# Backward pass of a segment-recurrent attention block: second dO half copied by two engines, tail block's fold moved to the dH fold, tail passes halved, hi parts first in folds

## The chip, the core and the metric

One core of a Trainium2 chip runs the whole program in one launch. The metric is device microseconds of an execution; the kernel before took 3185.75 us in the median of 4 runs (3175.45 to 3195.62). Profiles show one execution: the engines PE (matmul), PEld (its weight loads), DVE, ACT, POOL, and SP, which here only issues DMAs.

## The reference, cut to what matters

The program computes the output of a conditioned transformer block and the gradients of its eleven inputs. The block is layer norm with modulation, a memory-augmented attention over 64 segments of 32 rows each, and a gated MLP. What the change touches is the backward pass of the attention:

```python
for s in range(n_seg):                                   # 64 segments, in the backward pass from 63 down to 0
    h = jnp.concatenate([mem, xs], axis=1)               # 8 memory rows, 32 rows of x: L = 40
    q = jnp.einsum('btd,dhe->bhte', h, Wq)               # k, v likewise; 32 heads of 128
    p = _softmax(jnp.where(mask, einsum(q, k) * scale, -1e9), axis=-1)
    o = jnp.einsum('bhqk,bhke->bhqe', p, v)
    o = jnp.einsum('bhte,hed->btd', o, Wo)
    mem = o[:, :M, :].copy()                             # the next segment's memory
    outs.append(o[:, M:, :])
_out, _vjp = jax.vjp(_f, A_x, A_mem0, A_Wq, A_Wk, A_Wv, A_Wo, B_w_gate, B_w_up, B_w_down, c, w_mod)
```

The gradient of a segment's memory rows is part of the gradient of the output of the segment before it, so the backward pass is a chain of 64 segments.

## The kernel before

The program runs in phases: the forward attention (to about 1010 us of the profile), the MLP forward and backward, the backward attention (`phase4`, 1574 to 2570 us), and the weight gradients. The change is in `phase4` and in helpers that `phase4` calls. `fold_sum` and `TailRows` serve the forward attention's tail blocks too, once in four segments.

`phase4` is one loop over the segments s = 63 to 0. Its instruction order is written out by hand: `self.pin(i0)` keeps each engine in program order, so whatever stands behind a waiting instruction on its engine waits too. A step does this, by name:

- **dO pass.** `col_pass` multiplies the step's gradient columns `dyT` by `WoT`, in two halves `hf` of 16 matmuls; four column groups of PE work side by side. Each half lands in a PSUM tile `pass_ps` and is copied to the row tile `RAd`: half 0 by DVE, half 1 by ACT. POOL copies both on into `dOst` (L1538).
- **Turn.** `turn(0)` and `turn(1)` transpose `RAd` on PE (L1390), each in two tiles `turn_ps`, and ACT and DVE write them into `dOT`.
- **Gradients.** `gv0` and `gv1` are dV products (`grad_mm`, L1509, tiles `g_ps`); `dp`, `ds` give dS (L1488, L1496, L1498); `dost(2)` transposes part of `dOT` (L1424, tiles `tps`). `grad_out` copies a `g_ps` to `dVT`, `dKT` or `dQT`. After the third part, SP transposes the whole tile by DMA into `rows_x` (L1517), and POOL stores that to DRAM. The next step's first copy into `dVT` has to wait until that DMA has read it.
- **dH.** `dht` multiplies `dVT`, `dKT`, `dQT` by the transposed weights into `dh_ps` (L212, 96 matmuls). `fold_split` splits `dh_ps` into bf16 hi parts (ACT, L305) and lo parts (DVE, L309), two halves of 256 columns each, and `fold_sum` adds the four row groups up with 8 small matmuls into `dh_ft` (L318). ACT copies its memory rows into the next step's `dyT` (L1597), which the next dO pass needs.

Work of the **tail rows** (the last 8 rows of each segment, gathered for blocks of four segments) is put between these. `proj_b(t, hf)` is a dO pass over a block's tail rows `dyb`, half 0 in the steps with s % 4 = 3 and half 1 in those with s % 4 = 2, after the fold. `turn_b` transposes its result in the steps with s % 4 = 1. `TailRows` multiplies a block's tail gradients by the three weights (96 matmuls into `dh_tps`): `chunk()` runs one of four pieces of 24 matmuls in each step, between `fold_split` and `fold_sum`. `tail.split()` splits a finished block, in the steps with s % 4 = 3, and its `fold_sum` (`dh_b_ft`) runs in the `pop_later` between the `dKT` and the `dQT` products. `store_rows` copies `dh_ft` into `dh_tb` on DVE (L326) and turns it later (L330).

The loop's PSUM tiles share eight buffers (called banks below): six rotate under the tag "p" of the pool `psp`; `dh_ps` and `dh_tps` have one each, under tags of the pool `psb`. A tile of "p" gets a bank that an earlier tile has left, and its first matmul waits until that tile's last reader is done.

Of the kernel before, what the change touches and what calls it, by code (L numbers as in the profile page):

```python
# [40 lines left out]
class K:  # L41
# [199 lines left out]
    def col_pass(self, psp, w, hf, lhs, rows, eng):  # L241

        E, DC = self.cfg.E, self.cfg.DC
        ps = psp.tile([128, 512], F32, name="pass_ps", tag="p")
        for c in range(DC):
# [52 lines left out]
    def fold_split(self, pool, ps, name, tags=""):  # L298

        nc = self.nc  # L300
        parts = []
        for h in range(2):
            sl = slice(256 * h, 256 * h + 256)
            hi = pool.tile([128, 256], BF16, name=name + "_hi", tag=f"{tags}hi{h}", bufs=1)
            nc.scalar.activation(hi[:], ps[:, sl], AF.Copy)  # L305
            parts.append(hi)
        for h in range(2):
            lo = pool.tile([128, 256], BF16, name=name + "_lo", tag=f"{tags}lo{h}", bufs=1)
            nc.vector.tensor_tensor(lo[:], ps[:, 256 * h:256 * h + 256], parts[h][:], op=ALU.subtract)  # L309
            parts.append(lo)  # L310
        return parts

    def fold_sum(self, psp, parts, name, tag):

        ft = psp.tile([128, self.cfg.DC, 32], F32, name=name + "_ft", tag=tag)
        for c in range(self.cfg.DC):
            for i in range(2):
                self.nc.tensor.matmul(ft[:, c, :], lhsT=parts[2 * i + c // 2][:, (c % 2) * 128:(c % 2) * 128 + 128],  # L318
                                      rhs=self.foldsel[:], start=(i == 0), stop=(i == 1))
# [988 lines left out]
    def phase4(self):  # L1308
# [7 lines left out]
        with self.p4_ctx as ctx:  # L1316
# [76 lines left out]
            def proj_b(t, hf):  # L1393
                ps = self.col_pass(psp, WoT, hf, lambda c: dbs[t][:, c, :, :].rearrange("p s q -> p (s q)"), None, None)
                return lambda: self.evac(("act", "dve")[hf], RBds[t % 2][:, 512 * hf:512 * hf + 512], ps[:])
# [40 lines left out]
            for hf in range(2):  # L1436
                proj_b(NS // 4 - 1, hf)()
# [17 lines left out]
            tail = TailRows(self, sb2, psp, psb, 3, "dh", self.DHB, 4)  # L1455
            i0 = len(self.traced())
            for s in reversed(range(NS)):
# [78 lines left out]
                for hf in range(2):  # L1536
                    self.col_pass(psp, WoT, hf, lambda c: dyT[:, c, :], RAd, ("dve", "act")[hf])
                    nc.gpsimd.tensor_copy(dOst[0:96, 512 * hf:512 * hf + 512], RAd[0:96, 512 * hf:512 * hf + 512])  # L1538
                if pend:
# [14 lines left out]
                grad_out("dVT", dVT, 0, "act", gv0)  # L1554
                dost(2)
# [32 lines left out]
                if split:  # L1588
                    self.pop_later()
# [437 lines left out]
```

## Time and profile before

| | |
|---|---|
| median of 4 runs (range) | 3185.75 us (3175.45 to 3195.62) |
| the profiled execution | 3175.45 us, of which its span is 3173.5 us |
| PE busy in the span | 2977.2 us (94%), 39993 matmuls |
| DVE, ACT, POOL busy | 1586.5, 1159.5, 1481.2 us |
| `phase4` loop, 1574.4 to 2570.0 us: PE, DVE, ACT, POOL busy | 945.01, 506.06, 446.95, 455.21 us of 995.60 |
| the same: granted clock, DMA share, GB/s | 0.99, 1.11, 260 |

A matmul's end is modelled and matmuls overlap, so a PE that counts as busy can still stand still; waits inside a step are seen in the start times. The DMA share counts the time of all packets over 16 engines; packets of different queues overlap, so it can exceed 1.

### The profile page before, as it was taken

How to read it: one execution, taken by the hardware profiler on the slowest of the kernel's cores; microseconds unless marked ns; L12 is line 12 of the kernel's file. 1: busy time of each engine (PE TensorE's matmuls, PEld its weight loads, DVE VectorE, ACT ScalarE, POOL GpSimd, SP SyncE). 2: the span in 40 equal slices, each digit the busy share in tenths (PEclk: the TensorE clock that was granted, in tenths of full speed). 3: DMA queues.
4: the chain of work that ended last, by engine and by line, in shares of the span. 5: the costliest groups of instructions: out<-in, count | busy, mean ns of one | idle time of the engine just before them, and what ended most of it. 6: DMA issues, size and time to landing. Idle time of an engine off the chain costs nothing.

```text
span 3173.5 us, 98793 instructions
## 1 busy us (share of the span) xinstructions
PE 2977.2 (94%) x39993; PEld 1727.7 (54%) x40069; DVE 1586.5 (50%) x3770; ACT 1159.5 (37%) x2829; POOL 1481.2 (47%) x2973
## 2 busy tenths in 40 slices
PE   5999999999998799989999999999999969999999
PEld 3666666666665444445555555555555534455454
DVE  4666666666655777632245554555555421322221
ACT  2454454454454333312144444444444410100011
POOL 3666666666665466521244444444444421333322
PEclk8999999999999899999999999999999989999999
DMA  8888788788788798897599999999999999998986
GB/s 293 206 211 205 203 203 207 198 208 203 199 206 238 184 220 219 204 282 254 181 239 271 262 263 262 262 266 269 272 264 258 256 222 222 250 210 195 206 230 152
DMA packets 958892, 726.12 MB, mean 229 GB/s; under 512 B 656018, under 2 KB 831138, under 8 KB 958308
## 3 DMA queue, kind: packets, MB, share of 16 engines
q1 hardware_dynamic: 827940, 508.77, 70.6%
q0 software_dynamic: 59056, 148.62, 13.8%
q10 hardware_dynamic: 71440, 62.40, 7.8%
q8 instruction: 316, 5.18, 0.7%
q14 instruction: 140, 1.15, 0.1%
HBM read 294.91 MB, written 276.33 MB: 180 GB/s over the span
## 4 chain that ended last, share of the span: by engine, by line
PE 35%; issue 10%; DMA 6%; POOL 2%; ACT 2%; DVE 1%; SPq 1%; ACTq 0%; POOLq 0%; DVEq 0%
PE dh_ps L212 10%; PE gps L1820 5%; PE pass_ps L249 4%; PE g_ps L1509 3%; PE gps5o L1833 3%; PE dh_tps L212 3%; DMA rows<-DKR 2%; PE tps L1424 2%; PE dp_ps L1488 1%; DMA rows<-OSR 1%; PE dp_ps L1496 1%; ACT RAd L61 1%; PE dh_ft L318 1%; PE turn_ps L1390 1%; POOL out_dram L1824 1%
## 5 line engine op out<-in xcount | busy, mean ns | idle before, releaser
L1820 PE MATMUL gps<-rows,hrows 128*128 128x512 bf16 (+2 forms) x2124 | 415.7, 355 | 2.9 <-ACT ot L61 1.0
L1820 PEld LDWEIGHTS <-hrows 128*128 128x128 bf16 x2160 | 211.4, 98 | 205.5 <-issue 1.5
L249 PEld LDWEIGHTS <-hT 128*32 128x32 bf16 x6144 | 158.2, 97 | 161.3 <-issue 1.9
L1538 POOL COPY dOst<-RAd 96x512 bf16<-96x512 bf16 x128 | 78.6, 615 | 355.2 <-DVE RAd L63 343.9
L852 POOL TENSOR_TENSOR Pst<-Pst,rden 120x1408 bf16<-120x1408 bf16 x63 | 161.2, 2559 | 108.3 <-issue 76.7
L1824 POOL DMA_DIRECT2D out_dram<-ot x108 | 81.5, 755 | 232.7 <-DVE ot L63 137.5
L63 DVE CAST ot<-gps 128x512 bf16<-128x512 f32 (+3 forms) x76 | 47.8, 633 | 255.9 <-PE gps L1820 107.6
L309 DVE TENSOR_TENSOR dh_lo<-dh_ps,dh_hi 128x256 bf16<-128x256 f32 x128 | 48.4, 420 | 240.5 <-ACT dh_hi L305 240.5
L1833 PE MATMUL gps5o<-WoT,rows 128*128 128x512 bf16 x588 | 132.1, 384 | 25.5 <-DMA rows<-OSR 24.9
L61 ACT ACTIVATE ot<-gps 128x512 bf16<-128x512 f32 (+3 forms) x75 | 41.1, 548 | 282.9 <-PE gps L1820 134.4
L212 PE MATMUL dh_ps<-WvT,dVT 128*32 128x512 bf16 x2048 | 134.8, 382 | 0.0
L249 PE MATMUL pass_ps<-Wv,hT 128*32 128x512 bf16 x2048 | 133.3, 380 | 0.0
L1498 DVE SCALAR_TENSOR_TENSOR dS<-dp_ps,Pst_l 128x512 bf16<-128x512 f32 (+1 forms) x192 | 112.2, 640 | 33.4 <-PE dp_ps L1496 33.3
L249 PE MATMUL pass_ps<-WoT,dyT 128*32 128x512 bf16 x2048 | 123.5, 383 | 5.2 <-ACT dyT L1597 5.2
L220 PE MATMUL at_ps<-Wo,OT 128*32 128x256 bf16 x4096 | 124.8, 275 | 0.5 <-DVE OT L63 0.2
L249 PE MATMUL pass_ps<-Wk,hT 128*32 128x512 bf16 x2048 | 123.3, 383 | 1.5 <-ACT hT L842 1.1
L212 PE MATMUL dh_ps<-WqT,dQT 128*32 128x512 bf16 x2048 | 122.8, 379 | 0.1
L212 PE MATMUL dh_ps<-WkT,dKT 128*32 128x512 bf16 x2048 | 122.5, 380 | 0.0
L249 PE MATMUL pass_ps<-Wq,hT 128*32 128x512 bf16 x2048 | 121.6, 379 | 0.0
L63 DVE CAST RA0v<-pass_ps 128x512 bf16<-128x512 f32 x128 | 88.3, 690 | 65.4 <-PE pass_ps L249 59.9
L61 ACT ACTIVATE dVT<-g_ps 128x512 bf16<-128x512 f32 (+1 forms) x192 | 107.8, 562 | 35.6 <-PE g_ps L1509 20.6
L694 ACT ACTIVATE ET<-st_ps 128x480 bf16<-128x480 f32 (+1 forms) x192 | 96.1, 535 | 54.2 <-ACT qT L61 37.3
(411 smaller groups left out, 7033.7 us busy)
## 6 DMA issues: line engine op xcount, KB each, us to landing
OSR<-Ost SPq DMA_DIRECT2D x64, 352.0 KB
OT<-OT SPq DMA_DIRECT2D x64, 352.0 KB
VT<-VTr SPq DMA_DIRECT2D x64, 352.0 KB
PS<-Pst SPq DMA_DIRECT2D x64, 352.0 KB
OT_l<-OT SPq DMA_DIRECT2D x64, 352.0 KB
Pst_l<-PS SPq DMA_DIRECT2D x64, 352.0 KB
VT_l<-VT SPq DMA_DIRECT2D x64, 352.0 KB
DKR<-rows_x POOLq DMA_DIRECT2D x64, 352.0 KB, 6.0
```

Source lines behind the costliest of these rows:

```text
L61: return nc.scalar.activation(out, in_, AF.Copy)
L63: return nc.vector.tensor_copy(out, in_)
L212: self.nc.tensor.matmul(ps[32 * j:32 * j + 32, :], lhsT=lhsT, rhs=w, start=(n < 4), stop=(n >= total - 4), tile_position=(0, 32 * j))
L220: nc.tensor.matmul(ps[32 * j:32 * j + 32, :], lhsT=x[k], rhs=w[k][:, 256 * d:256 * d + 256], start=(n == 0), stop=(n == total - 1), tile_p ...
L249: self.nc.tensor.matmul(ps[32 * j:32 * j + 32, :], lhsT=lhs(c), rhs=rhs, start=(c == 0), stop=(c == DC - 1), tile_position=(0, 32 * j))
L694: nc.scalar.activation(part3(ET, pi)[:, 0:n, 0:120], st_ps[:, 0:n, 0:120], AF.Exp, scale=cfg.scale)
L852: nc.gpsimd.tensor_tensor(Pst[0:120, :, :], Pst[0:120, :, :], rden[:, :].unsqueeze(2).to_broadcast([120, G, 128]), op=ALU.mult)
L1498: nc.vector.scalar_tensor_tensor(out=part3(dS, pi), in0=ps[:, 0:n, :], scalar=cfg.scale, in1=part3(Pst, pi), op0=ALU.mult, op1=ALU.mult)
L1509: nc.tensor.matmul(ps[:, j, :], lhsT=lh[:, g * GW:(g + 1) * GW], rhs=rh[:, g * GW:(g + 1) * GW], start=True, stop=True)
L1820: nc.tensor.matmul(ps[:, 0:ng * E], lhsT=hrows[:, tp_, c * 128:(c + 1) * 128], rhs=rows[:, tp_, 0:ng * E], start=(tp_ == 0), stop=(tp_ == ...
L1824: nc.gpsimd.dma_start(outw[c * 128:(c + 1) * 128, h0:h0 + 3 * (ng - 1) + 1:3, :], ot[:, 0:ng * E].rearrange("p (h e) -> p h e", e=E))
L1833: nc.tensor.matmul(pss[gg][:], lhsT=rows[:, tp_, gg * E:(gg + 1) * E], rhs=dyrows[:, tp_, :], start=(tp_ == order[0]), stop=(tp_ == order[ ...
```

## The change

It has five parts. The copy of the second dO half is divided, columns 512 to 767 on ACT and 768 to 1023 on DVE. The tail block's `fold_sum` moves from between the `dKT` and `dQT` products to just ahead of the step's own `fold_sum`; its hi and lo parts get a place of their own in the tile `dS`. `proj_b` runs its first 8 matmuls of a half after the fold and the other 8 after the next step's dO pass, and takes the bank of `dh_ps` for that; the copy of its result comes after the first copy into `dVT` (ACT, in the steps with s % 4 = 2) or after the products `prod` on DVE (s % 4 = 1). The tail product's pieces become 16, 24, 24, 24 and 8 matmuls, the 8 standing behind the fold in the steps with s % 4 = 0. `fold_sum` runs its four hi matmuls before its four lo matmuls.

```diff
--- before.py
+++ after.py
@@ -238,11 +238,12 @@
                                       rhs=self.foldhalf[:, c // 2, :], start=(i == 0), stop=(i == 1))
         return ft
 
-    def col_pass(self, psp, w, hf, lhs, rows, eng):
+    def col_pass(self, psp, w, hf, lhs, rows, eng, ps=None, cs=None):
 
         E, DC = self.cfg.E, self.cfg.DC
-        ps = psp.tile([128, 512], F32, name="pass_ps", tag="p")
-        for c in range(DC):
+        if ps is None:
+            ps = psp.tile([128, 512], F32, name="pass_ps", tag="p")
+        for c in cs or range(DC):
             wc = w[:, c, :].rearrange("p (h e) -> p h e", e=E)
             for j in range(4):
                 rhs = wc[:, 12 * hf + j:12 * hf + j + 10:3, :] if j < 3 else wc[:, 24 + 4 * hf:28 + 4 * hf, :]
@@ -295,28 +296,31 @@
                 self.tc.add_manual_dep(ins, last[ins.engine].name, mybir.DependencyInfo(
                     mybir.DependencyClass.NoSync, mybir.DependencyReason.DATA), reason="program order")
 
-    def fold_split(self, pool, ps, name, tags=""):
+    def fold_split(self, pool, ps, name, home=None):
 
         nc = self.nc
         parts = []
-        for h in range(2):
-            sl = slice(256 * h, 256 * h + 256)
-            hi = pool.tile([128, 256], BF16, name=name + "_hi", tag=f"{tags}hi{h}", bufs=1)
-            nc.scalar.activation(hi[:], ps[:, sl], AF.Copy)
-            parts.append(hi)
-        for h in range(2):
-            lo = pool.tile([128, 256], BF16, name=name + "_lo", tag=f"{tags}lo{h}", bufs=1)
-            nc.vector.tensor_tensor(lo[:], ps[:, 256 * h:256 * h + 256], parts[h][:], op=ALU.subtract)
-            parts.append(lo)
+        for i, x in enumerate(("hi", "lo")):
+            for h in range(2):
+                if home is None:
+                    t = pool.tile([128, 256], BF16, name=f"{name}_{x}", tag=f"{x}{h}", bufs=1)[:, :]
+                else:
+                    t = home[:, 256 * len(parts):256 * len(parts) + 256]
+                sl = ps[:, 256 * h:256 * h + 256]
+                if i == 0:
+                    nc.scalar.activation(t, sl, AF.Copy)
+                else:
+                    nc.vector.tensor_tensor(t, sl, parts[h], op=ALU.subtract)
+                parts.append(t)
         return parts
 
     def fold_sum(self, psp, parts, name, tag):
 
         ft = psp.tile([128, self.cfg.DC, 32], F32, name=name + "_ft", tag=tag)
-        for c in range(self.cfg.DC):
-            for i in range(2):
+        for i in range(2):
+            for c in range(self.cfg.DC):
                 self.nc.tensor.matmul(ft[:, c, :], lhsT=parts[2 * i + c // 2][:, (c % 2) * 128:(c % 2) * 128 + 128],
-                                      rhs=self.foldsel[:], start=(i == 0), stop=(i == 1))
+                                      rhs=self.foldsel[:], start=(i == 0 and c == 0), stop=(i == 1), skip_group_check=True)
         return ft
 
     def store_rows(self, psp, pool, ft, dram, name, tag, then=None):
@@ -1390,9 +1394,21 @@
                         nc.tensor.transpose(tp[:, i, :], RAd[:, (i0 + i) * 128:(i0 + i + 1) * 128], self.ident[:, :])
                     to_heads(eng, tp[:], i0, 2, 0, 32, 0)
 
-            def proj_b(t, hf):
-                ps = self.col_pass(psp, WoT, hf, lambda c: dbs[t][:, c, :, :].rearrange("p s q -> p (s q)"), None, None)
-                return lambda: self.evac(("act", "dve")[hf], RBds[t % 2][:, 512 * hf:512 * hf + 512], ps[:])
+            def proj_b(t, hf, parts=1):
+                ps = psb.tile([128, 512], F32, name="pass_ps", tag="dh")
+
+                def part(k):
+                    self.col_pass(psp, WoT, hf, lambda c: dbs[t][:, c, :, :].rearrange("p s q -> p (s q)"), None, None, ps,
+                                  range(k * DC // parts, (k + 1) * DC // parts))
+
+                part(0)
+
+                def rest():
+                    for k in range(1, parts):
+                        part(k)
+                    return lambda: self.evac(("act", "dve")[hf], RBds[t % 2][:, 512 * hf:512 * hf + 512], ps[:])
+
+                return rest
 
             def turn_b(t):
                 tps = [self.turn_half(psp, RBds[t % 2], hf) for hf in range(2)]
@@ -1434,7 +1450,7 @@
             nc.vector.memset(dyT[:, :, 0:M], 0.0)
             get_loads(NS - 1)
             for hf in range(2):
-                proj_b(NS // 4 - 1, hf)()
+                proj_b(NS // 4 - 1, hf)()()
             turn_b(NS // 4 - 1)()
             to_heads("pool", btd[:], 0, 8, 32, 8, 24)
 
@@ -1452,7 +1468,8 @@
                 while len(row_stores) > left:
                     row_stores.pop(0)()
 
-            tail = TailRows(self, sb2, psp, psb, 3, "dh", self.DHB, 4)
+            b_rest = []
+            tail = TailRows(self, sb2, psp, psb, 3, "dh", self.DHB, (16, 24, 24, 24, 8), home=dSs[0])
             i0 = len(self.traced())
             for s in reversed(range(NS)):
                 i2 = s % 2
@@ -1534,8 +1551,14 @@
                         n_dh[0] += 1
 
                 for hf in range(2):
-                    self.col_pass(psp, WoT, hf, lambda c: dyT[:, c, :], RAd, ("dve", "act")[hf])
+                    ps = self.col_pass(psp, WoT, hf, lambda c: dyT[:, c, :], None, None)
+                    if hf == 0:
+                        self.evac("dve", RAd[:, 0:512], ps[:])
+                    else:
+                        self.evac("act", RAd[:, 512:768], ps[:, 0:256])
+                        self.evac("dve", RAd[:, 768:1024], ps[:, 256:512])
                     nc.gpsimd.tensor_copy(dOst[0:96, 512 * hf:512 * hf + 512], RAd[0:96, 512 * hf:512 * hf + 512])
+                b_done = b_rest.pop()() if b_rest else None
                 if pend:
                     pend.pop()()
                 store_rows_x(1)
@@ -1552,6 +1575,8 @@
                 dp(2)
                 gv1 = grad_mm("dVT", dOst, Pst, 1)
                 grad_out("dVT", dVT, 0, "act", gv0)
+                if b_done:
+                    b_done()
                 dost(2)
                 grad_out("dVT", dVT, 1, "act", gv1)
                 ds(0)
@@ -1585,19 +1610,19 @@
                 for pi in range(NP):
                     dht(dKT, WkT, pi)
                 dht(dVT, WvT, 2)
-                if split:
-                    self.pop_later()
                 for pi in range(NP):
                     dht(dQT, WqT, pi)
                 parts = self.fold_split(sb2, dh_ps[0], "dh")
                 tail.collect(s % nseg_t, [dVT, dKT, dQT])
                 tail.chunk()
+                if split:
+                    self.pop_later()
                 ft = self.fold_sum(psp, parts, "dh", "p")
                 if dyT_next is not None:
                     nc.scalar.activation(dyT_next[:, :, 0:M], ft[:, :, 0:M], AF.Copy)
                 if s > 3:
                     if s4 >= 2:
-                        proj_b(s // 4 - 1, 3 - s4)()
+                        b_rest.append(proj_b(s // 4 - 1, 3 - s4, 2))
                     elif s4 == 1:
                         turn_b(s // 4 - 1)()
                 then = None
@@ -1610,6 +1635,7 @@
 
                 pend.append(lambda ft=ft, s=s, then=then: self.store_rows(psp, sb2, ft, self.DHA[s], "dh", "p", then))
                 if s4 == 0:
+                    tail.chunk()
                     tail.begin(s, [WvT, WkT, WqT])
             pend.pop()()
             store_rows_x(0)
@@ -1877,9 +1903,9 @@
 
 
 
-    def __init__(self, k, pool, psp, psb, n, name, dram_b, npieces=4, tags=""):
+    def __init__(self, k, pool, psp, psb, n, name, dram_b, npieces=4, home=None):
         self.k, self.pool, self.psp, self.psb, self.n, self.name = k, pool, psp, psb, n, name
-        self.dram_b, self.npieces, self.tags = dram_b, npieces, tags
+        self.dram_b, self.npieces, self.home = dram_b, npieces, home
         self.cur = None
         self.pieces = []
         self.whole = None
@@ -1899,21 +1925,21 @@
         cfg, H = self.k.cfg, self.k.cfg.H
         tiles, self.cur = self.cur, None
         order = [(i, h) for i in range(self.n) for h in range(H)]
-        per = len(order) // self.npieces
+        sizes = self.npieces if isinstance(self.npieces, tuple) else self.npieces * (len(order) // self.npieces,)
         st = {}
 
         def piece(u):
             def f():
                 if u == 0:
                     st["ps"] = self.psb.tile([128, 512], F32, name=f"{self.name}_tps", tag="b")
-                for n in range(u * per, (u + 1) * per):
+                for n in range(sum(sizes[:u]), sum(sizes[:u + 1])):
                     i, h = order[n]
                     self.k.col_mm(st["ps"], tiles[i][:, h, :], ws[i][:, h, :], n, len(order))
-                if u == self.npieces - 1:
+                if u == len(sizes) - 1:
                     self.whole = st["ps"], s0
             return f
 
-        self.pieces = [piece(u) for u in range(self.npieces)]
+        self.pieces = [piece(u) for u in range(len(sizes))]
 
     def chunk(self):
         if self.pieces:
@@ -1923,7 +1949,7 @@
         if self.whole is None:
             return False
         (ps, s0), self.whole = self.whole, None
-        parts = self.k.fold_split(self.pool, ps, self.name + "_b", self.tags)
+        parts = self.k.fold_split(self.pool, ps, self.name + "_b", self.home)
 
         def summed():
             ft = self.k.fold_sum(self.psp, parts, self.name + "_b", "p")
```

## The prediction

> **What bounds the kernel now.** I read the page first (busy shares, DMA digits), then the waits inside the `phase4` loop, then the timeline of single steps.
>
> ```profile
> DMA  8888788788788798897599999999999999998986
> ```
> In the loop (the 21st to the 32nd slice) the DMA digit is 9 throughout, and so is PE's: two resources are full at once.
>
> ```profile
> PE turn_ps L1390 <- ACT RAd L61: 24.4, 64, 0.6
> PE pass_ps L249 <- ACT dyT L1597: 5.2, 18, 0.3
> ...
> PE dh_tp L330 <- ACT dVT L61: 1.1, 3, 0.5
> ACT dVT L61 <- DMA rows_x<-dVT: 11.8, 19, 1.6
> ```
> PE's largest wait is for the copy of the second dO half. The last row is DMA showing through: ACT's first copy into `dVT` waits for the transposing DMA of the step before, yet PE hardly notices (1.1 us). Modelled matmul ends hide more, so start times decide:
>
> ```profile
> 2290.07 1.90 PE L249 MATMUL pass_ps<-WoT,dyT 128*32 128x512 bf16 x32
> 2291.97 0.40 PE L1390 MATMUL turn_ps<-ident,RAd 128*128 128x128 bf16 x4
> 2292.73 0.40 PE L1390 MATMUL turn_ps<-ident,RAd 128*128 128x128 bf16 x4 [0.36 <-ACT RAd L61]
> ...
> 2294.18 0.33 PE L1424 MATMUL tps<-ident,dOT 128*128 128x128 bf16 x3
> ...
> 2294.96 0.22 PE L330 MATMUL dh_tp<-ident,dh_tb 128*128 128x128 bf16 x1
> ...
> 2292.08 0.60 ACT L61 ACTIVATE RAd<-pass_ps 128x512 bf16<-128x512 f32 x1 [2.58 <-PE pass_ps L249]
> ...
> 2293.45 0.60 ACT L61 ACTIVATE dVT<-g_ps 128x512 bf16<-128x512 f32 x1
> ...
> 2291.84 0.28 DVE L326 CAST dh_tb<-dh_ft 128x128 bf16<-128x128 f32 x1
> 2292.41 0.42 DVE L63 COPY dOT<-turn_ps 128x192 bf16<-128x192 bf16 x3 [0.29 <-PE turn_ps L1390]
> 2293.17 0.36 DVE L63 COPY dOT<-turn_ps 128x192 bf16<-128x192 bf16 x2 [0.34 <-PE turn_ps L1390]
> ```
> Four transposes issue in 0.22, so turn(1) could start at 2292.19; it starts at 2292.73: 0.54 lost. The next fence is the tail fold (2023.75 on), the same place in a step without it (2040.00), and the fold with what follows.
>
> ```profile
> 2023.75 0.60 PE L212 MATMUL dh_ps<-WvT,dVT 128*32 128x512 bf16 x8
> ...
> 2024.95 1.91 PE L212 MATMUL dh_ps<-WqT,dQT 128*32 128x512 bf16 x32
> ...
> 2040.00 0.60 PE L212 MATMUL dh_ps<-WvT,dVT 128*32 128x512 bf16 x8
> 2040.43 1.90 PE L212 MATMUL dh_ps<-WqT,dQT 128*32 128x512 bf16 x32
> ...
> 2302.76 0.66 ACT L305 ACTIVATE dh_hi<-dh_ps 128x256 bf16<-128x256 f32 x2 [2.72 <-PE dh_ps L212]
> ...
> 2303.45 0.76 DVE L309 TENSOR_TENSOR dh_lo<-dh_ps,dh_hi 128x256 bf16<-128x256 f32 x2 [4.07 <-ACT dh_hi L305]
> ...
> 2304.05 0.18 PE L318 MATMUL dh_ft<-foldsel,dh_hi 128*128 128x32 bf16 x1
> 2304.26 0.19 PE L318 MATMUL dh_ft<-foldsel,dh_lo 128*128 128x32 bf16 x1
> ...
> 2012.29 0.18 PE L318 MATMUL dh_ft<-foldsel,dh_lo 128*128 128x32 bf16 x1
> 2012.75 1.91 PE L249 MATMUL pass_ps<-WoT,dyT 128*32 128x512 bf16 x32 [0.29 <-ACT dyT L1597]
> ```
> From dO pass to dO pass an undisturbed step takes 16.06, 15.47, 14.82 and 14.73 us for s % 4 = 3, 2, 1, 0 (in the timeline for instance 2029.46 to 2044.93 and 2044.93 to 2059.75): 61.08 a cycle, 15.27 a step. The loop as it ran, first step aside, took 15.46.
>
> **The change, per cycle of four steps.**
>
> *Tail fold moved.* In its old place it costs (2024.95 - 2023.75) - (2040.43 - 2040.00) = 0.77 once a cycle. In the new one its parts are long ready and its 8 small matmuls (0.03 apart, 0.22) run while PE would wait for the second `dh_lo` anyway. With 16 tail matmuls there instead of 24 (0.43 less cover) PE arrives early and waits longer, but ends at the same `dh_lo`. **-0.77**; without that cover it would be -0.55.
>
> *Hi first.* PE stalls between 2304.05 and 2304.26 for the second `dh_lo`, with three matmuls behind it; now two are behind. About 0.045 in each of four steps: **-0.18**, ends 0 and -0.3.
>
> *proj_b halved.* Its 16 matmuls take 0.87 (2028.59 to 2029.46). Half, 0.43, leaves the fold in two steps: **-0.85**. What it covered there is the wait for `dyT`: 2012.75 - 2012.29 = 0.46 from the last fold matmul to the pass with nothing between; 8 matmuls and a start gap take about 0.5, so the cover holds. The other halves come back under the next term.
>
> *Turn, with divided copy.* ACT's 256 columns take 0.38 (`dh_hi`, same shape): 2292.08 to 2292.46. In the changed program's order DVE's half waits for ACT's, since both read one PSUM tile. The row for that is `dh_lo`: it starts at 2303.45, when the second `dh_hi` ends (2303.42), though it needs only the first. No row shows 256 columns as a cast on DVE; between `dh_tb` (128, 0.28) and a whole half (512, 0.69) I take 0.42, by width: 2292.49 to 2292.91. The second tile of turn(1) then starts near 2292.97 instead of 2292.84. `dh_tb` and five `dOT` copies follow on DVE and end near 2293.76 instead of 2293.53; part of `dp` waits on them. Followed through, `dp` ends 0.08 late. In two of the four steps 8 `proj_b` matmuls stand before turn(0): they push it 0.36 back, still before 2292.97, so they are free. **+0.32** for four steps; ends -0.8 (the two copies side by side) and +1.4 (DVE's half as dear as a whole one).
>
> The Trainium skill (PSUM — Partial Sum Buffer, PSUM bank collisions raise a hardware error) says that two engines must never touch one bank and quadrant at once, reads included, whatever the columns. It speaks against this copy: by the rule the halves run one after the other, as the `dh_lo` row shows. Without it turn(1) would start 0.2 sooner than now in the steps without `proj_b`, about 0.8 a cycle at most.
>
> *Tail product's 8 matmuls behind the fold at s % 4 = 0.* 0.5 against the 0.46 gap there: **+0.07**; ends 0 and +0.43.
>
> *Late copies of proj_b.* On ACT (s % 4 = 2) the 0.60 falls into the idle 0.56 ahead of the `dOst` copy: 0, at most 0.6 with `dVT` late. On DVE (s % 4 = 1) 0.69 stands behind `prod`, which ended at 2294.41 and now ends 0.2 later; dS is queued behind it and comes 0.4 later, which the 24 dH matmuls before PE's transposes of dS hide. But the first of those matmuls takes the copied bank: free near 2295.3, due near 2295.19 (it started at 2295.11), **+0.11**; ends 0 and 0.69.
>
> Sum: -0.77 - 0.18 - 0.85 + 0.32 + 0.07 + 0.11 = -1.30 a cycle; 15 cycles give **-19.5 us**. Steps become nearly even (14.8 to 15.1).
>
> *A new wait.* In the changed program's order the `tps` of `dost(2)` take the bank that `gv0` had; before, `dh_tp` did. So PE now needs the first `dVT` copy finished at 2294.18 instead of 2294.96, where it ended at 2294.05: the spare falls from 0.91 to 0.13. Behind `tps` queue `ds` and all of dH. Each late transposing DMA then reaches PE almost whole: of the 11.8 us that ACT waited, up to 11.8 - 19 x 0.13 = 9.3 us. At the low end it is nothing: a step in which PE waits once gives the DMA that time. POOL's second `dOst` copy, which waits for both halves, starts 0.2 later, with the DKR and DVR stores behind it, and SP waits for their buffers (79.0 us over the loop); SP's own order is the same. The DMA share of 1.11 says there is little to run faster with. I take 7.5 us for all of it, near the 9.3.
>
> So -19.5 + 7.5 = -12 us. The profiled execution (3175.45: its span 3173.5 and 1.95 around it) would become 3163.5. It is the fastest of the four; the others show no profile to explain their 5 to 20 us, so I take the -12 from the median, 3185.75: **3173**, own range 3164 to 3182.
>
> **Rivals.**
>
> *DMA gives nothing* (chance 0.15). If DMA needs 15.46 a step whatever PE does, all 19.5 return: 3186. For it: share 1.15 between 1889 and 2244 us, at 15.41 a step. Against: PE's DMA waits there are single events, with undisturbed steps between.
>
> *DMA follows* (0.25). Even steps ask less of it, the 12 us that the loop lost against 15.27 (0.19 x 62) partly vanish: -22 to -28, near 3161. For it: the 1.08 share between 2258 and 2427 us.
>
> *The new wait rules* (0.16), the slower side: `dVT` late in every step, with PE at `tps` each time. Now the mean lateness is 11.8 / 62 = 0.19 us. Shorter steps ask 0.33 earlier; with 0.2 more from POOL's later stores it is 0.72 late, less 0.13 spare: 0.59 x 62 = 37 us, net +17, 3203. It turns the sign from a lateness of 0.45 a step on (19.5 / 62 + 0.13).
>
> *The copy does run side by side* (0.02): 0.8 + 0.32 a cycle more, some -28 in all, 3158.
>
> **Chances.** Forecast 0.42. A measurement of this kernel can tell about 0.5% (16 us) from no change. Faster by more: the two gaining rivals and a fifth of the forecast, 0.35. Slower by more: 0.16. The rest, 0.49, within. The range 3154 to 3199 leaves out most of the slower case and the edge of the gaining ones.
>
> **What would show it.** Right: no `dh_b_ft` between `dKT` and `dQT`; turn(1)'s wait on DVE's `RAd` copy, which starts as ACT's ends; steps of 14.8 to 15.1; `tps` L1440 waiting for `dVT`, with a total near 7 us. Wrong: both `RAd` copies at once; `tps` waits above 20 us or steps still above 15.4; a gain outside 1574 to 2570 us.

## The result, and the profile after

| | median | range | against before |
|---|---|---|---|
| before, 72 runs | 3187.36 us | 3172.39 to 3198.64 | |
| after, 46 runs | 3178.69 us | 3168.67 to 3192.64 | 0.9977, 95% interval 0.9971 to 0.9984 |

The change gains 7.3 us (0.0023 x 3187; 5.1 to 9.2). The prediction was 12 us less, 3173 with an own range of 3164 to 3182. The size is near; the way to it is only partly the one predicted.

The profiled execution took 3173.23 us, 2.2 us less than that of before. Its loop from the first to the last dO pass is even 3.4 us longer (983.7 against 980.3 us), because this one execution has more late DMAs (the lost times below). The profiled execution of before lies 12 us under its median, that of after 5 us. So single executions are read here for what a step looks like, and ratios for what it is worth. The DMA row of the page has kept its shape:

```profile
DMA  8788888888889798897599999999999999998885
```

The waits inside the loop, profile after (us in total, times, longest):

```profile
PE turn_ps L1394 <- DVE RAd L63: 6.1, 35, 0.2
PE turn_ps L1394 <- ACT RAd L61: 3.7, 16, 0.4
PE pass_ps L250 <- ACT dyT L1622: 1.1, 4, 0.3
...
PE tps L1440 <- ACT dVT L61: 14.5, 18, 2.6
DVE RAd L63 <- ACT RAd L61: 38.3, 64, 0.9
ACT dVT L61 <- DMA rows_x<-dVT: 22.5, 20, 2.9
```

PE's 24.4 us at `turn_ps` are now 9.8, and 4.1 of the 5.2 us for `dyT` are gone. The new wait at `tps` is there, and ACT's wait for the transposing DMA of `dVT` has doubled (11.8 before). DVE waited for ACT's half of the copy in all 64 steps. A step without any late DMA (s = 20, dO pass at 2240.57), timeline after:

```profile
2242.42 0.40 PE L1394 MATMUL turn_ps<-ident,RAd 128*128 128x128 bf16 x4
2242.59 0.38 ACT L61 ACTIVATE RAd<-pass_ps 128x256 bf16<-128x256 f32 x1 [1.48 <-PE pass_ps L250]
2243.01 0.42 DVE L63 CAST RAd<-pass_ps 128x256 bf16<-128x256 f32 x1 [0.65 <-ACT RAd L61]
2243.03 0.29 PE L1394 MATMUL turn_ps<-ident,RAd 128*128 128x128 bf16 x2 [0.22 <-ACT RAd L61]
2243.49 0.29 PE L1394 MATMUL turn_ps<-ident,RAd 128*128 128x128 bf16 x2 [0.17 <-DVE RAd L63]
2243.78 0.13 PEld L1526 LDWEIGHTS <-dOst 128*128 128x128 bf16 x2 [0.18 <-issue]
2243.81 0.22 PE L1526 MATMUL g_ps<-Pst_l,dOst 128*128 128x128 bf16 x1
2244.28 0.60 ACT L61 ACTIVATE dVT<-g_ps 128x512 bf16<-128x512 f32 x1 [0.42 <-POOL dOst L1560]
2244.93 0.33 PE L1440 MATMUL tps<-ident,dOT 128*128 128x128 bf16 x3
2245.71 0.22 PE L334 MATMUL dh_tp<-ident,dh_tb 128*128 128x128 bf16 x1
```

The halves run one behind the other, 0.38 and 0.42 us, as priced. The second tile of turn(1) starts 2.92 us after the dO pass (predicted 2.90). But `tps` comes 4.36 and `dh_tp` 5.14 us after it; before it was 4.11 and 4.89. `tps` starts 0.05 after the first `dVT` copy ends at 2244.88, so it is bound by that copy even here.

The start of `gv0` (`g_ps`) is compared with before below. Its row there, in the step that the prediction reads (turn(1) at 2292.73, dO pass at 2290.07):

```profile
2292.97 0.39 PE L1509 MATMUL g_ps<-Pst_l,dOst 128*128 128x128 bf16 x4
```

The fold of the step s = 19, where the tail fold now stands, timeline after:

```profile
2268.57 0.66 ACT L311 ACTIVATE dh_hi<-dh_ps 128x256 bf16<-128x256 f32 x2 [2.22 <-PE dh_ps L212]
2269.25 0.37 PE L322 MATMUL dh_b_ft<-foldsel,dS 128*128 128x32 bf16 x8
2269.26 0.76 DVE L313 TENSOR_TENSOR dh_lo<-dh_ps,dh_hi 128x256 bf16<-128x256 f32 x2 [2.12 <-ACT dh_hi L311]
2269.47 0.25 PE L322 MATMUL dh_ft<-foldsel,dh_hi 128*128 128x32 bf16 x4
2269.74 0.55 PE L322 MATMUL dh_ft<-foldsel,dh_lo 128*128 128x32 bf16 x4
2270.22 0.62 PE L250 MATMUL pass_ps<-WoT,dyb 128*32 128x512 bf16 x8
```

The eight `dh_b_ft` matmuls run while the second `dh_lo` is being made (to 2270.02), eight `proj_b` matmuls in place of 16 follow: as predicted.

**Clean steps and lost time.** The step lengths split into two parts that the whole study needs. The clean length is the shortest that recurs among the 13 steps of a kind (s = 55 to 4); what the mean is above it is time lost to waits that come and go, by the waits' rows mostly for DMAs. Ratios are against before, with the 95% interval; us are (ratio - 1) x 3187.

| kernel | ratio | us | clean, s % 4 = 3, 2, 1, 0 | sum | lost at s % 4 = 2 |
|---|---|---|---|---|---|
| before | | | 16.06, 15.47, 14.82, 14.73 | 61.08 | 0.31 |
| after | 0.9977 (0.9971 to 0.9984) | -7.3 | 15.07, 15.26, 14.94, 15.02 | 60.29 | 1.08 |
| e1 whole copy | 0.9960 (0.9949 to 0.9971) | -12.7 | 14.84, 15.13, 14.80, 14.79 | 59.56 | 1.77 |
| e2 other bank | 0.9947 (0.9928 to 0.9966) | -16.9 | 15.01, 15.26, 15.00, 15.02 | 60.29 | 1.06 |
| e3 two dVT, after | 0.9983 (0.9970 to 0.9996) | -5.4 | 15.02, 15.21, 15.00, 14.97 | 60.20 | 0.63 |
| e4 two dVT, before | 1.0015 (0.9996 to 1.0035) | +4.8 | 16.00, 15.53, 14.82, 14.67 | 61.02 | 0.58 |
| e5 e1, daq spread | 0.9993 (0.9977 to 1.0009) | -2.2 | 14.84, 15.13, 14.79, 14.79 | 59.55 | 2.49 |
| e6 e2, daq spread | 0.9978 (0.9961 to 0.9996) | -7.0 | 15.01, 15.26, 14.99, 15.02 | 60.28 | 1.57 |
| e7 before, daq spread | 0.9995 (0.9980 to 1.0010) | -1.6 | 16.06, 15.47, 14.82, 14.73 | 61.08 | 0.55 |
| e8 before, divided copy | 0.9994 (0.9981 to 1.0008) | -1.9 | 16.29, 15.76, 15.05, 14.96 | 62.06 | 0.07 |
| e9 before, tail fold moved | 0.9987 (0.9972 to 1.0001) | -4.1 | 15.30, 15.59, 14.82, 14.73 | 60.44 | 0.57 |
| e10 before, proj_b halved | 0.9964 (0.9947 to 0.9981) | -11.5 | 15.62, 15.03, 14.82, 14.73 | 60.20 | 1.41 |
| e11 e2 without daq | 0.9922 (0.9898 to 0.9947) | -24.9 | 15.01, 15.26, 14.99, 15.02 | 60.28 | 0.20 |
| e12 e2, daq behind the loads | 0.9942 (0.9924 to 0.9961) | -18.5 | 15.01, 15.26, 14.99, 15.02 | 60.28 | 0.39 |

The lost times come from one execution each; the other three kinds of steps lost 0.0 to 0.9 us. Clean lengths repeat to 0.01 us. The executions are not equally typical: that of before is 12 us faster than its median, that of e12 the fastest of its six, that of e1 the slowest of its eleven. So the 0.31 of before is likely low: e7, whose time is that of before, lost 0.55. The part of the program outside the loop also differs between the 14 executions, by up to 15 us (2187.8 to 2202.9).

### The profile page after: what moved, and what is told of

The parts are those of the page before. It is cut to its first block, busy times and chain, and to the rows that moved or that the text cites. A ratio compares the mean times of both kernels' runs of the same rounds, so it can differ in the third digit from the quotient of the medians.

```text
span 3171.5 us, 98880 instructions
## 1 busy us (share of the span) xinstructions
PE 2981.9 (94%) x39993; PEld 1729.9 (55%) x40069; DVE 1593.3 (50%) x3834; ACT 1148.6 (36%) x2829; POOL 1481.3 (47%) x2973
## 5 line engine op out<-in xcount | busy, mean ns | idle before, releaser
L63 DVE CAST RAd<-pass_ps 128x512 bf16<-128x512 f32 (+1 forms) x128 | 71.4, 558 | 130.1 <-PE pass_ps L250 91.8
```

The source lines that it names most:

```text
L63: return nc.vector.tensor_copy(out, in_)
```

## The experiments

My theory at the start (A) was the prediction's sum: the edits shorten PE's work, and the new bank wait gives part back. Its rivals: the divided copy costs far more than priced (B); DMA sets the pace (C).

**e1 and e2: the two halves of the divided copy's price.** Both start from the kernel after. e1 copies the half whole again:

```diff
-                        self.evac("act", RAd[:, 512:768], ps[:, 0:256])
-                        self.evac("dve", RAd[:, 768:1024], ps[:, 256:512])
+                        self.evac("act", RAd[:, 512:1024], ps[:])
```

> The kernel after with the second dO half copied whole by ACT again. With it, the tps of dost(2) are again given the bank of the last turn_ps, and dh_tp the bank of gv0: two things of the change are undone at once. Theory A (the prediction's sum): the divided copy cost 0.32 a cycle, 4.8 us, and the new wait 7.5 us, so this kernel takes 12 us less than after, near 3166, ratio to before 0.993 to 0.994. Rival B (the divided copy itself costs more than priced: the two traces show gv0 0.2 to 0.3 us later in its step after than before; the new wait costs nothing): 0.2 x 62 = 12 us less as well, ratio 0.993 to 0.994; e2 tells A from B. Rival C (DMA sets the pace of the loop, whatever PE does): as after, ratio 0.997 to 0.998.

e2 keeps the divided copy and puts the three transposes of `dost(2)` into the last `turn_ps` tile:

```diff
-                    tp = psp.tile([128, 2, 128], BF16, name="turn_ps", tag="p")
                     i0 = 4 * hf + 2 * k
+                    tp = room[0] = psp.tile([128, 2 if i0 < 6 else 5, 128], BF16, name="turn_ps", tag="p")
...
-                ps = ps_b16("tps")
+                ps = ps_b16("tps") if w == GW else room[0][:, 2:5, :]
```

> The kernel after with the divided copy kept, but with the three transposes of dost(2) written into free columns of the last turn_ps tile, so that tps no longer takes the bank that gv0 had; dh_tp takes it, as in the kernel before. Only the new wait is undone. Theory A: 7.5 us less than after, ratio to before near 0.995, and PE waits for dVT at dh_tp with a few us at most in place of 14.5 us at tps. Rival B: as after within 2 us, ratio 0.997 to 0.998. Rival C: as after. The difference between e1 and this kernel is the price of the divided copy alone: 4.8 us by A, some 12 us by B.

Measured: e1 -12.7 us, e2 -16.9 us. e2 is 9.6 us faster than after (0.9977 - 0.9947; 3 to 16 us with both intervals). Its clean steps are those of after, so the whole difference lies in late steps. Waits in e2's loop:

```profile
ACT dVT L61 <- DMA rows_x<-dVT: 20.1, 19, 2.6
...
PE dh_b_tp L334 <- ACT dVT L61: 5.0, 6, 1.4
...
PE dh_tp L334 <- ACT dVT L61: 0.3, 1, 0.3
```

`dVT` is as late as in after (20.1 against 22.5 us), yet PE waits 5.3 us for it in place of 14.5: what a later due time is worth. The new wait was real, and its 7.5 us were about right. The difference that I had set down as the copy's own price is not there: e1 is 4 us slower than e2 (3 us faster to 11 slower), although its clean cycle is 0.73 us shorter. Rival B is right on the clean steps: 0.13 to 0.23 us a step. Where the whole copy loses it again is in the last column: e1 loses 1.77 us in the mean step with s % 4 = 2, e2 1.06.

**e3 and e4: a second dVT tile.** In both kernels two `dVT` tiles alternate. e3 is built on after, e4 on before; the fold parts lie in `dST` (in e4 the tail's in `dS` as well), and `dh_b_tb` and `dh_b_rb` have one buffer in place of two. No run has these rearrangements without the second `dVT`.

```diff
-            dXTs = {nm: ptiles(nm, n, zero=False) for nm, n in (("dVT", 1), ("dKT", 1), ("dQT", 1))}
+            dXTs = {nm: ptiles(nm, n, zero=False) for nm, n in (("dVT", 2), ("dKT", 1), ("dQT", 1))}
...
-                dVT, dKT, dQT = dXTs["dVT"][0], dXTs["dKT"][0], dXTs["dQT"][0]
+                dVT, dKT, dQT = dXTs["dVT"][s % 2], dXTs["dKT"][0], dXTs["dQT"][0]
...
-                parts = self.fold_split(sb2, dh_ps[0], "dh")
+                parts = self.fold_split(sb2, dh_ps[0], "dh", dSTs[0])
```

> The kernel after with two dVT tiles that alternate, so that ACT's first copy into dVT no longer waits for the transposing DMA of the step before (22.5 us over the loop in the profile of after). To make room, the hi and lo parts of the step's own fold lie in the tile dST, and dh_b_tb and dh_b_rb have one buffer instead of two. Theory A: the wait for a late dVT is what reached PE at tps: 7.5 us less than after (ratio to before near 0.995), and up to 14.5 us less if all of PE's wait at tps was this. Rival B: 0 to 2 us less. Rival C: nothing, because what DMA doesn't get there it takes at another wait (POOL's stores, SP's buffers, the loads for g_ps), ratio 0.997 to 0.998.

> The kernel before with the same two dVT tiles (parts of both folds in dST and dS, one buffer for dh_b_tb and dh_b_rb). ACT waited 11.8 us for the DMA there, and PE 1.1 us for dVT at dh_tp. Theory A: about 1 us less than before, ratio 0.999 to 1.000. Rival C: no change. A gain of over 5 us (ratio below 0.9985) would say that late DMAs already reached PE in the kernel before by a way that I have not seen, and that the 7.5 us of the prediction were not new.

Measured: e3 -5.4, e4 +4.8 us. ACT no longer waits for the transposing DMA, the `tps` wait is gone, and nothing is gained. Waits in e3's loop:

```profile
PE g_ps L1526 <- DMA dOst<-RBd: 12.1, 5, 5.0
PE g_ps L1526 <- DMA Kst<-KST: 8.3, 6, 2.5
```

In after these were 8.2 and 1.0 us. The mean step over s = 55 to 4 is 15.58 us in both profiles. The 7.5 us of theory A are not there (e3 is 2 us slower than after, 3 faster to 6 slower), and C fits: `dVT` is only the first place where PE meets a DMA that is behind; take it away and PE meets the next one. The rearrangements may have a price of their own: e4, which has them on before, came out 4.8 us slower (1 us faster to 11 slower). That I did not follow up.

**e5, e6, e7: where the late DMA comes from.** All kernels that shorten the step with s % 4 = 3 lose in the step after it. That step holds one more load, `daq`, and the trace's DMA events give the transposing DMA of `dVT` there 7.48 us from issue to landing in e1 (median of 14), 5.8 to 6.6 in the others. (In before it takes 7.10 us there too; what the change moves is when `dVT` is due.) So theory D: spread that load.

```diff
-                if s4 == 3:
+                if s == NS - 1:
                     get_da(s // 4 - 1)
+                elif s4 == 3:
+                    self.get_da_part(s // 4 - 1, 3, 1)
+                elif s4 == 0:
+                    self.get_da_part(s // 4 - 2, 1, 2)
...
                 load_rows(Kst_t, self.KST, s - 1)
+                if s4 == 1:
+                    self.get_da_part(s // 4 - 2, 0, 1)
```

> e1 (the kernel after with the whole copy on ACT) with the load of daq, 128 KB once a cycle in the step with s % 4 = 3, divided: one quarter late in the step with s % 4 = 1, two in s % 4 = 0, one in s % 4 = 3. Theory D: in the step with s % 4 = 3 this load makes the transposing DMA of dVT slow (issue to landing 7.5 us there in e1, 6.0 to 6.6 in the other steps); before, that step was the longest and hid it; the change shortens just this step by 1 us, and ACT's first dVT copy of the step with s % 4 = 2 comes late. In e1's profile the steps with s % 4 = 2 lose 1.7 us over their clean 15.06, the others 0.2 to 0.5. By D most of the 1.7 goes: 1.2 x 15 = 18 us less than e1, ratio to before near 0.990 (0.988 to 0.993), and the rows_x<-dVT DMA of s % 4 = 3 takes 6 to 6.8 us. Rival C (the loop's DMA needs its time whatever the order; bytes are the same): as e1, ratio 0.995 to 0.997, the loss only moves to other steps. Rival E (two more DMAs a cycle on SP's queue cost more than they bring): slower than e1, above 0.997.

> e2 (the kernel after with tps in the bank of the last turn_ps) with the daq load divided as in e5. In e2's profile the steps with s % 4 = 2 lose 1.0 us over their clean 15.26, the others 0.0 to 0.3. Theory D: some 0.7 x 15 = 10 us less than e2, ratio to before near 0.9915 (0.990 to 0.994). Rival C: as e2, 0.994 to 0.996. The difference to e5 is the divided copy with its DMA free again: clean steps of e1 are 0.2 us shorter (59.48 against 60.29 a cycle), so e5 should be 6 to 12 us faster than e6 if D holds, and equal or slower if C holds.

> The kernel before with the daq load divided as in e5. There the steps with s % 4 = 2 lost only 0.29 us over their clean length. Theory D: the long step hid the load, so little is to be had: 0 to 4 us, ratio 0.9987 to 1.000. If this kernel gains as much as e5 does over e1 (over 10 us, ratio below 0.997), the load was no cost of the change but one that both kernels had, and D is wrong on the change. Rival C: 1.000.

Measured: e5 -2.2, e6 -7.0, e7 -1.6 us: e5 and e6 are each 10 us slower than e1 and e2, and the loss at s % 4 = 2 grew. D as I put it falls, rival E holds, but only where the steps have been shortened: in before the same three pieces cost nothing that can be measured (e7, 0.9980 to 1.0010). In e5 a quarter in the step with s % 4 = 3 took 4.5 us to land, the whole load in e1 4.3. A load in pieces is not lighter here; `VT_l`, the last load behind it, was issued 5.43 us into that step in place of 4.95, and 5.01 in place of 4.0 with s % 4 = 0, and the transposing DMA of `dVT` in the former took 8.29 us. The Trainium skill (Perfetto Trace Analysis, DMA Optimizations) says that splitting DMAs may let a task finish sooner if the DMA engines are generally idle; the DMA digit of 9 says that they are not, and e5 and e6 show the other side of that rule.

**e8, e9, e10: three parts of the change alone,** each on the kernel before. e8:

```diff
-                    self.col_pass(psp, WoT, hf, lambda c: dyT[:, c, :], RAd, ("dve", "act")[hf])
+                    if hf == 0:
+                        self.col_pass(psp, WoT, hf, lambda c: dyT[:, c, :], RAd, "dve")
+                    else:
+                        ps = self.col_pass(psp, WoT, hf, lambda c: dyT[:, c, :], None, None)
+                        self.evac("act", RAd[:, 512:768], ps[:, 0:256])
+                        self.evac("dve", RAd[:, 768:1024], ps[:, 256:512])
```

> The kernel before with nothing but the divided copy of the second dO half. With it tps takes the bank of gv0, so the new wait comes along. The prediction's terms: +4.8 us for the copy and +7.5 us for the wait, at most 12 us slower, ratio near 1.004. With the clean steps of e1 and after (59.48 and 60.29 a cycle, so 0.2 us a step for the copy, 12.5 us) and e2's 9 us for the wait: 21 us slower, ratio near 1.0065. Rival C: longer steps give the DMA time, so the cost stays hidden: within 3 us, 0.999 to 1.001.

Measured: -1.9 us (-6.1 to +2.5). Every clean step is 0.23 to 0.29 us longer, 0.98 a cycle, 14.7 us over 15 cycles, and the kernel is no slower. The steps with s % 4 = 2 lose 0.07 us. Waits in e8's loop:

```profile
ACT dVT L61 <- DMA rows_x<-dVT: 9.3, 8, 1.8
PE tps L1424 <- ACT dVT L61: 5.2, 9, 1.2
```

This fits rival C: while PE is held up, DMA catches up. ACT waits 9.3 us for the transposing DMA, in before 11.8; the bank wait, 14.5 us in after, is 5.2 us here. But the two profiles don't show where the 14.7 us come back: before's execution is an unusually fast one, and e8's, at its median, has a loop of 990.2 us against 980.3. That DMA gave them back is inferred from the times.

e9 moves the tail fold (its parts in `dS`):

```diff
-                if split:
-                    self.pop_later()
                 for pi in range(NP):
                     dht(dQT, WqT, pi)
...
                 tail.chunk()
+                if split:
+                    self.pop_later()
```

> The kernel before with nothing but the tail fold moved to the step's own fold (its parts in dS; pieces of 24 as before). The prediction's term: 0.77 a cycle, 0.55 without cover, so 8 to 12 us less, ratio 0.996 to 0.9975; the clean steps with s % 4 = 3 go from 16.06 to 15.3. Rival C, now narrower (a shorter step with s % 4 = 3 makes dVT's transposing DMA late in the step behind it, which gives time back): the clean steps shorten all the same, but the steps with s % 4 = 2 lose 0.3 to 0.6 us more over their clean length than before (0.29), and the gain is half, 3 to 6 us, 0.998 to 0.999.

e10 halves `proj_b` (`proj_b` and `col_pass` as in the change):

```diff
-                proj_b(NS // 4 - 1, hf)()
+                proj_b(NS // 4 - 1, hf)()()
...
+                b_done = b_rest.pop()() if b_rest else None
...
                 grad_out("dVT", dVT, 0, "act", gv0)
+                if b_done:
+                    b_done()
...
-                        proj_b(s // 4 - 1, 3 - s4)()
+                        b_rest.append(proj_b(s // 4 - 1, 3 - s4, 2))
```

> The kernel before with nothing but the halved passes of proj_b (bank of dh_ps, late copies). The prediction's terms: -0.85 + 0.11 a cycle, 11 us less, ratio near 0.9965; clean steps 15.6 and 15.05 for s % 4 = 3 and 2 in place of 16.06 and 15.47. Rival C: half of it, 0.998 to 0.999, with more lost over the clean steps at s % 4 = 2.

Measured: e9 -4.1 us (-8.9 to +0.3), e10 -11.5 us (-16.9 to -6.1). Clean steps: e9 shortens s % 4 = 3 by 0.76 (0.77 priced) and lengthens s % 4 = 2 by 0.12, not foreseen; e10 shortens both its steps by 0.44. In time e9 fits the halved gain of rival C, e10 the prediction. At s % 4 = 2 e10 loses more than before and than e7 (1.41 against 0.31 and 0.55); e9's 0.57 is that of e7.

**e11 and e12: daq left out, and daq moved back.** Both are built on e2. e11 leaves 14 of the daq loads out, so part of its output is not that of the reference:

```diff
                 if s4 == 3:
                     get_da(s // 4 - 1)
+                    self.das.setdefault(s // 4 - 2, self.das.get(s // 4 - 1))
```

> e2 (the kernel after with tps in the bank of the last turn_ps) with 14 of the daq loads left out: each block of four segments uses the rows that the block before it had, so part of the data is not that of the reference. e5 and e6 showed that the daq load in more pieces costs 8 to 10 us, though the bytes are the same: the pieces landed as late as the whole, and OT_l, Pst_l and VT_l behind them were issued 0.5 to 1.0 us later. Theory F (each further DMA ahead of the loads on SP's queue makes these, and the transposing DMAs behind them, later): without daq the steps with s % 4 = 2 lose 0.3 us instead of 1.0 to 1.3 and those with s % 4 = 3 nothing: 10 us less than e2, ratio near 0.9915. Rival C in bytes (128 KB of some 16 MB a cycle): at most 8 us, no place named. Rival G (the loss at s % 4 = 2 has nothing to do with daq): as e2, 0.9935 to 0.996, and the loss at s % 4 = 2 stays near 1 us.

e12 only changes the order, with the copy into `dyb` moved to match:

```diff
-                if s4 == 3:
-                    get_da(s // 4 - 1)
                 ld = get_loads(s)
                 if s > 0:
                     get_loads(s - 1)
+                if s4 == 3:
+                    get_da(s // 4 - 1)
```

> e2 with the daq load issued behind OT_l, Pst_l and VT_l in the step with s % 4 = 3 instead of ahead of them, and POOL's copy into dyb moved behind dO_tails; nothing is left out. Theory F: the three loads are issued 0.45 us earlier there, while daq itself is not needed before 14 us of the step; 2 to 6 us less than e2, ratio 0.993 to 0.994, loss at s % 4 = 2 below 1 us. Rivals C and G: as e2, 0.9945 or 0.995. A version that beats both kernels either way, if e2's time holds.

Measured: e11 -24.9 us, e12 -18.5 us. In the profiles the loss at s % 4 = 2 goes from 1.06 to 0.20 and 0.39 us, and the transposing DMA of `dVT` with s % 4 = 3 from 6.58 us to 6.06 and 5.61. SP's queue in e2 from Kst on, step s = 31, and ACT in the next step:

```profile
2073.06 0.73 SPq L1447 DMA_DIRECT2D Kst<-KST  x1
2073.88 0.39 SPq L1247 DMA_DIRECT2D daq<-DAOT  x1
2074.33 0.49 SPq L1430 DMA_DIRECT2D OT_l<-OT  x1
2074.87 0.42 SPq L1430 DMA_DIRECT2D Pst_l<-PS  x1
2075.34 1.84 SPq L1433 DMA_DIRECT2D VT_l<-VT  x1
2078.61 0.34 SPq L1447 DMA_DIRECT2D Qst<-QST  x1
2080.80 2.92 SPq L1536 DMA_TRANSPOSE rows_x<-dKT  x1
2083.83 3.57 SPq L1536 DMA_TRANSPOSE rows_x<-dVT  x1
...
2091.55 0.60 ACT L61 ACTIVATE dVT<-g_ps 128x512 bf16<-128x512 f32 x1 [2.56 <-DMA rows_x<-dVT]
```

The same in e12:

```profile
2073.57 0.39 SPq L1430 DMA_DIRECT2D OT_l<-OT  x1
2074.00 0.42 SPq L1430 DMA_DIRECT2D Pst_l<-PS  x1
2074.46 0.44 SPq L1433 DMA_DIRECT2D VT_l<-VT  x1
2075.00 0.51 SPq L1247 DMA_DIRECT2D daq<-DAOT  x1
...
2079.99 2.35 SPq L1536 DMA_TRANSPOSE rows_x<-dKT  x1
2082.45 3.68 SPq L1536 DMA_TRANSPOSE rows_x<-dVT  x1
...
2088.93 0.60 ACT L61 ACTIVATE dVT<-g_ps 128x512 bf16<-128x512 f32 x1 [0.16 <-POOL dOst L1562]
```

SP issues everything in one line. In this step the transposing DMAs are issued 0.6 and 1.2 us sooner after the dO pass in e12 (it is at 2070.54 in e2, 2070.32 in e12), and `dVT` is free in time. The long issue of `VT_l` (1.84 us in e2, 0.44 in e12; the medians of 13 such steps are 0.43 and 0.44) is not the reason: it was over at 2077.18, and SP then waited for PE ahead of `Qst` and for the landing of POOL's store of `rows_x` into `DKR` ahead of `rows_x<-dKT`, until 2080.75 in e2 and 2079.94 in e12.

Nor is the step typical. In the median of 14 cycles the transposing DMA of `dVT` is issued no sooner in e12, 12.88 us after the dO pass against 12.70; it takes less time from issue to landing. What the loss at s % 4 = 2 follows is the place of that landing in the next step. Counted from the next dO pass, its median is 3.31 us in before, 3.84 in after, 4.79 in e1, 4.31 in e2, 5.13 in e5, 3.38 in e11 and 3.31 in e12; ACT's copy is due at about 3.4 with the whole copy (before, e1, e5) and at 3.6 in the others. So theory F holds for the place of the loss, though not by a later issue as it had it, and rival G fits worse, as far as one execution each can tell. Why the DMA lands sooner with `daq` behind the loads stays open. In the time it is not settled either: e11 and e2 have intervals that overlap, and e12 (0.9942) is not told apart from e2 (0.9947). Both e2 and e12 beat before and after.

## Why the prediction was right, and where it was not

- *Tail fold, proj_b, hi first, the tail's 8 matmuls.* Predicted together, with the late copies: -1.62 a cycle. e1, which has all of them without the divided copy, measures 61.08 - 59.56 = -1.52. The fold is -0.76 at its place (e9), `proj_b` -0.88 (e10): the +0.11 for the copy on DVE did not appear, 14.82 stayed 14.82. Hi first was not run alone; the steps of e1 that hold little else (14.82 to 14.80) leave it nearer 0.02 than 0.045.
- *Divided copy.* This is the term that was mis-sized: +0.32 predicted, +0.73 in after against e1 and +0.98 in e8 measured. The copies themselves and turn(1) came as worked out; "Followed through, `dp` ends 0.08 late" is the step that failed. Before, `gv0` started 0.24 after turn(1), with four transposes between. In after it starts 0.32 after the second tile, with only two: the `PEld` row at 2243.78 shows 0.18 idle with "issue", and by the semaphores' times all that `gv0` waits for had come before. The trace's sequencer rows have three semaphore instructions of `gv0` there, at 2243.49, 2243.60 and 2243.70; in e1 they stand at 2251.22 and 2251.33, beside the transposes that start at 2251.21. A wait in the middle of turn(1) pushes them behind it. Their number fits the delay: in undisturbed steps of after `gv0` starts 0.32 after the second tile where it has three of them (s % 4 = 3 and 0), 0.21 where it has two (s % 4 = 2 and 1), and 0.11 in before and e1, where they stand beside running transposes. Against e1 the clean steps of the first two kinds are 0.23 longer, of the other two 0.13 and 0.14; in e8 all four kinds have three and are 0.23 to 0.29 longer than before. So in the step shown `gv0` starts 3.24 us after the dO pass in place of 2.91, and `tps` 0.24 later than before. Of this the wait for the `dVT` copy is 0.06: in e2, without that wait, `tps` comes 4.30 after the dO pass in such a step.
- *The Trainium skill* (PSUM — Partial Sum Buffer, PSUM bank collisions raise a hardware error) was weighed against this copy. The profile agrees with the serial order (DVE starts 0.04 after ACT ends; DVE waited in 64 of 64 steps); the order is a wait in the program, so no run shows what two readers at once would do.
- *The new wait.* +7.5 predicted, 9.6 (3 to 16) by e2, 14.5 as a sum of waits. Its place and cause were right, and its size within what e2 can tell.
- *DMA.* The prediction let late DMAs return time at `tps` alone. The runs show that this is too narrow: the clean sums foretell the time only in some kernels (e8 +14.7 clean, -1.9 measured; e1 -22.8 clean, -12.7; e9 -9.6 clean, -4.1; but e10 -13.2 clean, -11.5, and e2 -11.9 clean, -16.9), and without the `dVT` wait (e3) PE waits elsewhere. What the rival "DMA gives nothing" describes is true of about half of the gain in e1 and e9, and mostly in the step behind the one with s % 4 = 3; in e10 and e2 none of it shows.
- *The sum.* Clean steps -0.79 x 15 = -11.9 in place of -19.5, the wait +9.6 in place of +7.5: -2.3, where -7.3 (-9.2 to -5.1) was measured. The 5 us between lie within the interval of e2. That the forecast came out near is in part luck: the copy lengthened the clean steps by 6 to 10 us more than priced (0.41 to 0.66 x 15), and most of this does not show in the times. That the DMA paid it back is the reading that fits e8 best, not one that a run isolates.

Signs named ahead: no `dh_b_ft` between `dKT` and `dQT`, and the serial copies, came; steps of 14.8 to 15.1 came for three kinds, 15.26 for s % 4 = 2; the `tps` total was 14.5, between "near 7" and "above 20", and the mean step of the profile was above 15.4, a sign named for wrong. It was, as far as one execution goes. Another such sign, a gain outside the loop, cannot be judged: in this pair of executions 5.6 us come from outside it, but the eight kernels that have the change's code there average 2192.2 us outside the loop and the six others 2194.8, in a spread of 15.

Left open: why e3, with no `dVT` wait at all, is slower than e2 (0.9983 against 0.9947), and the 0.12 that e9 adds at s % 4 = 2. No run takes away the order between the two `RAd` halves, or between two readers of one bank.

## What to carry to other kernels

Where two resources are full, split each step into its clean length and what is lost above it, kind by kind; an edit that shortens PE's part can be worth less than its clean gain where the DMA of that step is already the later one (e1 and e9 kept about half, e10 nearly all). Before shortening a step, see what else is queued in it: here the step that gave most had an extra load at the head of SP's queue, and the loss came in the step behind it. And when a tile pool chooses the bank, look up after every edit whose reader the next tile waits for: a copy cut in two changed that choice, which alone cost 9.6 us (3 to 16).

## What the runs showed of the hardware that was not expected

- The time that an issue holds SP's queue varies at equal size: `VT_l` took 0.44 us in e12 and 1.84 in e2 in the step shown, 0.43 to 1.84 over e2's 13 steps of that kind; the transposing DMAs of the rows shown took 2.35 to 3.68. That full DMA engines are the cause is my reading.
- A load of a quarter of the size, in the same place, landed no sooner (4.5 us against 4.3), and three loads in place of one made the changed kernels 10 us slower at equal bytes (e5 4 to 17, e6 2 to 18), but before no slower (e7).
- The semaphore instructions in which PE waits for several semaphores stand about 0.11 us apart when they come directly behind a stall, though by the semaphores' times all of them had been met (after, s = 20): `gv0` started 0.21 us after the tile behind the stall with two of them and 0.32 with three. Where two of them stand beside running transposes (before, e1) it started 0.11 after that tile.
- Lengthening every step of a full loop by 0.23 to 0.29 us cost nothing that can be measured (e8, 0.9981 to 1.0008).
